# A retention layer with a mixture of adapters: 64-token chunks, attention products on four 64x64 array tiles, pairs of units in a fixed program order

## The chip, the core and the metric

The kernel runs on one core of one Trainium2 chip. A core has five engines with queues of their own: PE (TensorE, matrix products; the loads of its stationary operand are listed as PEld), DVE (VectorE), ACT (ScalarE), POOL (GpSimd) and SP (SyncE, which here issues nearly all DMA transfers). SBUF is the working memory of 128 partitions; PE writes its results to PSUM, 8 banks of 512 fp32 values a partition. PE's array can be addressed as one 128x128 array, as two tiles (64 rows x 128 columns, or 128 x 64) or as four 64x64 tiles[...]. The metric is the device time of one execution in microseconds (us); lower is better.

## What is computed

Inputs q, k and v have 8 batches, 8 heads, 576 tokens and 64 elements a head, in fp32. Head h decays with its own gamma. The result of all heads is a row of 512 per token, and a mixture of 8 adapters of rank 16, the best two of them per token, is added to it.

```python
scores = np.matmul(q, k.transpose(0, 1, 3, 2)) / np.sqrt(64)
gamma = 1.0 - 2.0 ** (-5.0 - np.arange(8))
rel = pos[:, None] - pos[None, :]
Dmat = np.where(rel >= 0, gamma[:, None, None] ** rel, 0.0)
ret = np.matmul(scores * Dmat, v)
x = ret.transpose(0, 2, 1, 3).reshape(4608, 512)

logits = x @ w_gate                      # 512 x 8
topk = the two largest of 8 per token
w = softmax over these two
out = x + sum over the two: w * (x @ A[e]) @ B[e]     # A: 512 x 16, B: 16 x 512
```

## The kernel before

The 576 tokens are cut into four chunks of 128 and one of 64. Within a chunk the products are done directly (scores, a triangular mask, times v); what earlier chunks contribute is held in a state P of 64 x 64 per batch and head, which is multiplied by gamma^128 after each chunk. The decays are folded into q (tile `aqp`) and v (`gv`), so the mask is of zeros and ones (`tri`).

A unit is one chunk of two batches with all 8 heads: 16 full units of 128 tokens (order: chunk by chunk, four pairs of batches each) and 4 half units of 64 tokens at the end. Each unit passes these stages, each a function:

- `stage_T` (L229): q and k are transposed on PE by a product with a 64x64 identity, in the mode of two 64x128 tiles. The results are taken out of PSUM to qT by DVE (times `aqp`, L241) and to kT by ACT (L250).
- `stage_S` (L291, L302): scores, keys by queries, 128 x 128 for each head and batch, contracting over 64 elements: two 64x128 tiles. DVE masks them to `rt`.
- `stage_O` (L359, L373, L387): the state times q into `px` (four 64x64 tiles, 128 columns wide), and the new state product k by v into `pu` (two 128x64 tiles). DVE adds the old state (`pn`), POOL multiplies by the decay (L388). In half units the state times q goes into a tile of its own, `pq` (L341), and ACT copies it.
- `stage_R` (L408): v times the masked scores, added in PSUM to `px` (two 128x64 tiles); ACT copies `px` to `xT`. For half units this is L426, on four 64x64 tiles.
- `stage_Z` (L447): gate logits and all adapters' first products, `pz`, on the whole array; then routing on DVE (L460 to L479) with a sigmoid on ACT (L468) between, which ends in `zc`, the weighted codes in fp16.
- `stage_X`, `stage_B`, `stage_Y` (L493, L512, L533): codes transposed, `xT` transposed back into `po`, and the adapters' second product added to it in PSUM; ACT takes `po` out (L543) and SP stores it.

POOL scales v in place for a unit ahead (L197). Loads come in groups of four batches (`issue_full`, L127; 1 MB each of q, k and v, in runs of 256 bytes); each kind has three buffers of 1 MB, so a group's buffers are those of the group three before.

The order of the work is not the program's: the framework's scheduler orders the instructions on each engine by its own costs. So a transpose or a state product can be placed between products that wait for DVE. The 8 PSUM banks are one pool; a tile takes a bank that has come free and waits for its last reader.

The loop that the program states is this:

```python
    for t in range(NU):
        if t % 2 == 0:
            issue(t // 2 + 2)
        stage_S(t)
        if t + 1 < NU:
            scale_v(t + 1)
        stage_O(t)
        stage_R(t)
        if t + 1 < NU:
            stage_T(t + 1)
        if t > 0:
            stage_B(t - 1)
            stage_X(t - 1)
        stage_Z(t)
        if t > 0:
            stage_Y(t - 1)
```

Of the kernel before, what the change touches and what calls it, by code (L numbers as in the profile page):

```python
# [10 lines left out]
FP32 = mybir.dt.float32  # L11
# [7 lines left out]
def kernel(  # L19
# [28 lines left out]
    tri_np = (jj[None, :] >= jj[:, None]).astype(np.float32)  # L48
# [5 lines left out]
    for hp in range(HP):  # L54
# [11 lines left out]
        [ident32_np, tri_np, trih_np, gv_np, gvh_np, g128_np], axis=1  # L66
# [20 lines left out]
    tri = pack[:, 128:256]  # L87
    trih = pack[:, 256:320]
    gv = pack[:, 320 : 320 + H]
    gvh = pack[:, 320 + H : 320 + 2 * H]  # L90
    g128 = pack[:, 320 + 2 * H : 320 + 2 * H + HP]
# [19 lines left out]

    nat = {}

    def issue_full(c, qd, split):
        tiles = []
        for src, tag in ((q, "q32"), (k, "k32"), (v, "v32")):
            tiles.append((src, iop.tile([128, QUAD * H, Dh], FP32, tag=tag, name=tag)))
        parts = ((0, 2), (2, 4)) if split else ((0, 4),)
        for lo, hi in parts:
            for src, tl in tiles:  # L120
                if split and lo == 0 and src is k:
                    nc.sync.dma_start(out=aqp, in_=dr_aqp.ap())
                if split and lo == 0 and src is v:
                    nc.sync.dma_start(out=pack, in_=dr_rest.ap())
                if split and lo == 2 and src is q:
                    load_moe()
                nc.sync.dma_start(  # L127
                    out=tl[:, lo * H : hi * H, :],
                    in_=src[
                        QUAD * qd + lo : QUAD * qd + hi, :, 128 * c : 128 * c + 128, :  # L130
                    ].rearrange("b h j d -> j (b h) d"),
                )
        for half in range(2):
            nat[(c, 2 * qd + half)] = [
                tl[:, half * 2 * H : half * 2 * H + 2 * H, :] for _, tl in tiles
            ]

    def issue_half(qd):

        s0 = 128 * NFULL  # L140
        tiles = []
        for src, tag in ((q, "q32"), (k, "k32"), (v, "v32")):
            tiles.append((src, iop.tile([128, QUAD * H, Dh], FP32, tag=tag, name=tag)))
        for slot in range(2):
            for src, tl in tiles:
                for par in range(2):
                    b = QUAD * qd + 2 * slot + par
                    nc.sync.dma_start(
                        out=tl[64 * par : 64 * par + LH, slot * H : slot * H + H, :],
                        in_=src[b, :, s0 : s0 + LH, :].rearrange("h j d -> j h d"),  # L150
                    )
            nat[(NFULL, 2 * qd + slot)] = [
                tl[:, slot * H : slot * H + H, :] for _, tl in tiles
            ]

    quads = [(c, qd) for c in range(NFULL + 1) for qd in range(NQ)]

    def issue(n):
        if n < len(quads):
            c, qd = quads[n]  # L160
            if c < NFULL:
                issue_full(c, qd, n == 0)
            else:
                issue_half(qd)

    issue(0)

    issue(1)
    nc.vector.tensor_copy(out=ident16, in_=ident32)
    gdec = cpool.tile([128, HP, 2, Dh], FP32, tag="gdec", name="gdec")  # L170
# [4 lines left out]
    P = [  # L175
        cpool.tile([128, HP, 2, Dh], FP32, tag=f"P{bp}", name=f"P{bp}")
        for bp in range(NP)
    ]

    def swap_aw():  # L180
        for ho in range(2):
            nc.gpsimd.tensor_copy(
                out=AW[1][64 * ho : 64 * ho + 64],
                in_=AW[0][64 - 64 * ho : 128 - 64 * ho],
            )

    units = [(c, 2 * qd + s) for c, qd in quads for s in range(2)]
    st = {}

    def scale_v(t):  # L190
        c, bp = units[t]
        full = c < NFULL
        v32 = nat[(c, bp)][2]
        nb = 2 if full else 1
        g = gv if full else gvh
        for b in range(nb):
            nc.gpsimd.tensor_tensor(  # L197
                out=v32[:, b * H : b * H + H, :],
                in0=v32[:, b * H : b * H + H, :],
                in1=g.unsqueeze(2).broadcast_to((128, H, Dh)),  # L200
                op=ALU.mult,
            )

    def stage_T(t):
        c, bp = units[t]
        full = c < NFULL
        q32, k32, v32 = nat[(c, bp)]
        qT = wk.tile([128, HP, 2, 128], FP32, tag="qT", name="qT")
        kT = wk.tile([128, HP, 2, 128], FP32, tag="kT", name="kT")
        L = 128 if full else LH  # L210
        for src, dst, nm in ((q32, qT, "q"), (k32, kT, "k")):
            dv = dst.rearrange("p a b i -> p a (b i)")[:, :, 0 : 2 * L].rearrange(
                "p a (b i) -> p a b i", i=L
            )
            if full:
                ps = [
                    pp.tile([128, HP, 2, 64], FP32, tag="pb", name=f"pt_{nm}")
                    for _ in range(2)
                ]
            else:  # L220
                ps = [
                    pp.tile([128, HP, 64], FP32, tag="pb", name=f"pt_{nm}")
                    for _ in range(2)
                ]
            for hp in range(HP):
                for b in range(2 if full else 1):
                    for r in range(2):
                        sl = slice(64 * r, 64 * r + 64)
                        nc.tensor.matmul(  # L229
                            ps[r][:, hp, b, :] if full else ps[r][:, hp, :],  # L230
                            lhsT=src[sl, b * H + 2 * hp : b * H + 2 * hp + 2, :],
                            rhs=id64[sl, :],
                            is_transpose=True,
                            start=True,
                            stop=True,
                        )
            for r in range(2):
                if full:
                    o = dv[:, :, :, 64 * r : 64 * r + 64]
                    if nm == "q":  # L240
                        nc.vector.tensor_tensor(  # L241
                            out=o,
                            in0=ps[r],
                            in1=aqp[:, :, 64 * r : 64 * r + 64]
                            .unsqueeze(2)
                            .broadcast_to((128, HP, 2, 64)),
                            op=ALU.mult,
                        )
                    else:
                        nc.scalar.copy(out=o, in_=ps[r])  # L250
                else:
                    o = dv[:, :, r, :]
                    if nm == "q":
                        nc.vector.tensor_tensor(
                            out=o, in0=ps[r], in1=aqp[:, :, 0:64], op=ALU.mult
                        )
                    else:
                        nc.scalar.copy(out=o, in_=ps[r])
        view = lambda tl: tl.rearrange("p a b i -> p a (b i)")[:, :, 0 : 2 * L].rearrange(
            "p a (b i) -> p a b i", i=L  # L260
        )
        st[t] = {"qT": view(qT), "kT": view(kT), "v": v32, "k": k32}

    def stage_S(t):
        c, bp = units[t]
        full = c < NFULL
        s = st[t]
        qT, kT = s["qT"], s["kT"]
        L = 128 if full else LH
        rt = {}  # L270
        hpg = 2 if full else 4
        for g in range(HP // hpg):
            ps = [
                pp.tile(
                    [128, hpg, 2, 128] if full else [128, hpg, LH],
                    FP32,
                    tag="pb",
                    name=f"ps_s{ho}",
                )
                for ho in range(2)  # L280
            ]
            for a in range(hpg):
                hp = g * hpg + a
                for b in range(2):
                    for ho in range(2):
                        sl = slice(64 * ho, 64 * ho + 64)
                        if full:
                            o = ps[ho][:, a, b, :]
                        else:
                            o = ps[ho][64 * b : 64 * b + 64, a, :]  # L290
                        nc.tensor.matmul(  # L291
                            o,
# [6 lines left out]
            for ho in range(2):  # L299
# [16 lines left out]
                for a in range(hpg):  # L316
                    rt[2 * (g * hpg + a) + ho] = r[:, a, :, :]
# [293 lines left out]
```

## Time and profile before

| | |
|---|---|
| median of 3 runs | 207.6 us (207.38 to 208.12) |
| span of the profiled execution, from the first to the last instruction | 205.1 us |
| mean granted PE clock | 0.995 |
| HBM read, written | 29.32 MB, 9.44 MB |
| mask L302, DVE, 128x512 | 64 times, 682 ns |
| q scaling L241, DVE, 128x512 | 32 times, 686 ns |
| new state L387, DVE, 128x512 | 12 times, 691 ns |
| copy of `px` L417 and of k L250, ACT, 128x512 | 32 times each, 585 and 589 ns |
| output copy L543, ACT, 128x256 | 72 times, 375 ns |
| scaling of v L197, POOL, 128x512 | 36 times, 1042 ns |
| decay of the state L388, POOL, 128x512 | 16 times, 1271 ns |
| store of 256 KB, issue to landing | 3.2 us |
| DMA share and rate, 50 to 60 us | 0.97, 277 GB/s |
| the same, 150 to 160 us | 0.52, 137 GB/s |

The median is of separate runs; the durations come from one profiled execution, whose span leaves out what lies before its first and after its last instruction. A group's mean is the duration of one instruction by itself; two of them in a row overlap a little (two copies of k take 1.07 us together). PE's matmuls overlap far more, so that their pace is read from the distance of their starts, or from the chain of waits, and not from their mean durations.

### The profile page before, as it was taken

The page shows a single profiled execution, that of the slowest core. Times are in us where ns is not written, and L with a number is a line of the kernel's source. Part 1 is how long each engine was busy: PE and PEld are TensorE (multiplying, and loading weights), DVE is VectorE, ACT ScalarE, POOL GpSimd, SP SyncE. Part 2 cuts the span into 40 slices and gives each one's busy share as a digit, 9 for nine tenths or more (in the row PEclk, how much of TensorE's full clock was granted, in tenths as well). Part 3 has the DMA queues.
Part 4 walks back from the last instruction along what each step waited for, and adds up shares of the span by engine and source line. Part 5 has one row for each costly group of instructions (what it writes and reads, how often), then busy time and mean ns, then how long its engine had stood idle before and what let it go on. Part 6 is the DMA issues. An engine that isn't in the chain of part 4 may idle for free.

```text
span 205.1 us, 8039 instructions
## 1 busy us (share of the span) xinstructions
PE 183.8 (90%) x3564; PEld 166.2 (81%) x3564; DVE 108.7 (53%) x286; ACT 76.6 (37%) x206; POOL 59.6 (29%) x60
## 2 busy tenths in 40 slices
PE   0476989799999999999999999999999999999950
PEld 0376969598999999999999999999999899888830
DVE  0226364937374746465656565656565655456630
ACT  2022324153525262625252525253434344454430
POOL 1144323521818202727202720643222402000000
PEclk9999999999999999999999999999999999999997
DMA  5989999799998988991799969756545311222222
GB/s 114 277 109 246 249 243 280 194 290 290 253 319 245 261 249 274 284 297 36 220 286 254 266 215 293 213 145 179 150 118 158 96 51 60 101 79 76 58 47 61
DMA packets 57442, 39.14 MB, mean 191 GB/s; under 512 B 30912, under 2 KB 52672, under 8 KB 57408
## 3 DMA queue, kind: packets, MB, share of 16 engines
q1 hardware_dynamic: 57264, 38.50, 68.0%
q8 instruction: 28, 0.46, 0.9%
q0 software_dynamic: 144, 0.13, 0.4%
q14 instruction: 6, 0.05, 0.1%
HBM read 29.32 MB, written 9.44 MB: 189 GB/s over the span
## 4 chain that ended last, share of the span: by engine, by line
PE 72%; SPq 9%; DVE 7%; DMA 5%; ACT 3%; issue 1%; ACTq 0%
PE pz L447 16%; PE px L408 12%; PE ps_s L291 12%; PE pu L373 6%; PE px L359 6%; PE pt_q L229 5%; DMA k<-in_k_dram 5%; PE po L512 4%; SPq L127 4%; PE pt_k L229 4%; PE po L533 3%; DVE rt L302 2%; PE px L426 2%; ACT osb L543 2%; SPq L101 2%; PE pzt L493 2%
## 5 line engine op out<-in xcount | busy, mean ns | idle before, releaser
L197 POOL TENSOR_TENSOR v<-v,pack 128x512 f32<-128x512 f32 x36 | 36.6, 1042 | 28.0 <-DMA v<-in_v_dram 28.0
L417 ACT COPY xT<-px 128x512 f32<-128x512 f32 x32 | 18.7, 585 | 66.0 <-PE px L408 66.0
L388 POOL TENSOR_TENSOR P<-pn,gdec 128x512 f32<-128x512 f32 x16 | 20.3, 1271 | 75.3 <-DVE pn L387 58.9
L302 DVE TENSOR_TENSOR rt<-ps_s,pack 128x512 f32<-128x512 f32 x64 | 39.7, 682 | 4.2 <-PE ps_s L291 4.2
L291 PE MATMUL ps_s<-qT,kT 64*128 64x128 f32 (+1 forms) x640 | 37.4, 275 | 1.2 <-ACT kT L250 1.2
L447 PE MATMUL pz<-AW,xT 128*128 128x136 f32 x288 | 37.8, 283 | 0.4 <-ACT zT L498 0.4
L291 PEld LDWEIGHTS ps_s<-qT,kT 64*128 64x128 f32 (+1 forms) x640 | 33.7, 184 | 5.3 <-DVE lg L460 3.4
L241 DVE TENSOR_TENSOR qT<-pt_q,aqp 128x512 f32<-128x512 f32 x32 | 20.6, 686 | 31.1 <-PE pt_q L229 31.1
L408 PE MATMUL px<-rt,v 128*64 128x128 f32 x512 | 34.1, 275 | 1.8 <-DVE rt L302 1.7
L447 PEld LDWEIGHTS pz<-AW,xT 128*128 128x128 f32 x288 | 34.7, 190 | 0.6 <-ACT zT L498 0.5
L543 ACT COPY osb<-po 128x256 f32<-128x256 f32 x72 | 23.1, 375 | 25.8 <-PE po L533 25.8
L408 PEld LDWEIGHTS px<-rt,v 128*64 128x64 f32 x512 | 29.0, 137 | 3.8 <-DVE rt L302 2.5
L250 ACT COPY kT<-pt_k 128x512 f32<-128x512 f32 x32 | 17.2, 589 | 19.2 <-PE pt_k L229 19.2
L460 DVE COPY lg<-pz 128x16 f32<-128x16 f32 (+1 forms) x20 | 3.5, 173 | 35.0 <-PE pz L447 35.0
L229 PE MATMUL pt_q<-id,q 64*128 64x64 f32 x288 | 13.6, 234 | 6.7 <-DMA q<-in_q_dram 6.7
L373 PE MATMUL pu<-v,k 128*64 128x64 f32 x512 | 18.9, 225 | 0.0
L373 PEld LDWEIGHTS pu<-v,k 128*64 128x64 f32 x512 | 16.5, 137 | 2.7 <-issue 2.1
L229 PEld LDWEIGHTS pt_q<-id,q 64*128 64x128 f32 x288 | 10.8, 142 | 9.6 <-issue 9.4
L229 PE MATMUL pt_k<-id,k 64*128 64x64 f32 x288 | 12.8, 228 | 3.4 <-DMA k<-in_k_dram 3.4
L473 DVE SCALAR_TENSOR_TENSOR cm<-lg,m,sg 128x8 f32<-128x8 f32 x36 | 9.9, 294 | 8.8 <-ACT sg L468 8.8
L229 PEld LDWEIGHTS pt_k<-id,k 64*128 64x128 f32 x288 | 10.9, 143 | 3.8 <-issue 1.7
L359 PE MATMUL px<-qT,P 64*64 64x128 f32 x384 | 13.2, 275 | 0.0
(34 smaller groups left out, 139.9 us busy)
## 6 DMA issues: line engine op xcount, KB each, us to landing
out_dram<-osb SPq DMA_DIRECT2D x32, 256.0 KB, 3.2
q<-in_q_dram SPq DMA_DIRECT2D x2, 512.0 KB, 5.0
k<-in_k_dram SPq DMA_DIRECT2D x2, 512.0 KB, 6.0
v<-in_v_dram SPq DMA_DIRECT2D x2, 512.0 KB, 5.4
q<-in_q_dram SPq DMA_DIRECT2D x8, 128.0 KB, 3.4
k<-in_k_dram SPq DMA_DIRECT2D x8, 128.0 KB, 3.3
v<-in_v_dram SPq DMA_DIRECT2D x8, 128.0 KB, 4.1
out_dram<-osb SPq DMA_DIRECT2D x8, 128.0 KB, 2.4
```

Of the source, the lines that this page charges most:

```text
L197: nc.gpsimd.tensor_tensor(out=v32[:, b * H : b * H + H, :], in0=v32[:, b * H : b * H + H, :], in1=g.unsqueeze(2).broadcast_to((128, H, Dh) ...
L229: nc.tensor.matmul(ps[r][:, hp, b, :] if full else ps[r][:, hp, :], lhsT=src[sl, b * H + 2 * hp : b * H + 2 * hp + 2, :], rhs=id64[sl, :], ...
L241: nc.vector.tensor_tensor(out=o, in0=ps[r], in1=aqp[:, :, 64 * r : 64 * r + 64] .unsqueeze(2) .broadcast_to((128, HP, 2, 64)), op=ALU.mult,)
L291: nc.tensor.matmul(o, lhsT=kT[sl, hp, b, :], rhs=qT[sl, hp, b, :], start=(a == 0 and (b == 0 or not full)), stop=True, skip_group_check=True,)
L302: nc.vector.tensor_tensor(out=r.rearrange("p a b i -> p (a b) i"), in0=ps[ho].rearrange("p a b i -> p (a b) i"), in1=tri.unsqueeze(1).broa ...
L359: nc.tensor.matmul(px[b][64 * cc : 64 * cc + 64, hp, :], lhsT=P[bp][64 * ho : 64 * ho + 64, hp, b, :], rhs=qT[64 * ho : 64 * ho + 64, hp, ...
L373: nc.tensor.matmul(pu[64 * ho : 64 * ho + 64, hp, b, :], lhsT=s["k"][:, b * H + h, :], rhs=s["v"][:, b * H + h, :], start=(hp == 0 and b = ...
L388: nc.gpsimd.tensor_tensor(out=pf, in0=pn, in1=gdec.rearrange("p a b d -> p (a b d)"), op=ALU.mult,)
L408: nc.tensor.matmul(px[b][64 * cc : 64 * cc + 64, hp, :], lhsT=s["v"][:, b * H + h, :], rhs=rt[h][:, b, :], start=(c == 0 and hp == 0), sto ...
L417: nc.scalar.copy(out=xt, in_=px[b])
L447: nc.tensor.matmul(pz[:, b, :], lhsT=xts[b][:, dt, :], rhs=AW[b][:, dt, :], start=(dt == 0), stop=(dt == HP - 1), skip_group_check=True,)
L543: nc.scalar.copy(out=osb[:, b, :, cc ^ b, :], in_=po[cc][:, b])
```

## The change

Every group of four batches of a 128-token chunk is now worked on as a pair of units (A and B, two batches each), and the last 64 tokens of all eight batches are a single pair. There is one chunk loop of nine rounds; the loads of a round lie two rounds ahead.

Within a 128-token chunk the work is cut into two halves of 64 tokens, s = 0 and 1. Each half has its own scores (64 x 64), its own state product, and a state of its own: P for the first half, and p1 = P + the first half's product for the second (`mid_state`); `end_state` adds the second half's product. So the scores between the halves are no longer formed, and in their place is a state product more. Contractions and outputs are all 64 wide: scores, state product, values times scores and state times q run on four 64x64 tiles with 64 columns each, twice as many instructions as before. The half tokens' pair uses the same functions without the state product.

A round goes through three array modes: four 64x64 tiles for all attention products of A and B, then two 64x128 tiles for the transposes of the next pair and of the previous pair's output, then the whole array for the codes' transposes, the gates and the adapters. The context `tc.manual_schedule()` keeps each engine's instructions in the program's order.

The state times q is now added after the values, into the same banks from other row tiles; for this a copy of one column by ACT (`see`) waits for the values, and the first product of the state waits for it. The copy `xT` interleaves the tokens of the two batches (i, b), so that a tile holds 64 tokens of two batches, and a store of 256 KB goes to 64 rows of each batch.

The routing writes the sigmoid's argument for both halves in one instruction (`ar`), so one sigmoid and one `zc` serve a unit where there were two. The 128 x 128 mask is dropped from the constants; k's first half is loaded ahead of the constants, and the second half of the first group ahead of the adapters' weights.

The core of the diff; the old stage functions, which stand above, are left out:

```diff
+    order = ctx.enter_context(tc.manual_schedule())
+    groups = [(c, qd) for c in range(NFULL) for qd in range(NQ)] + [(NFULL, 0)]
...
+    def stage_S(u):
+        ps = [
+            pp.tile([128, HP, 2, 64], FP32, tag="pb", name=f"ps_s{ho}") for ho in range(2)
+        ]
+        for hp in range(HP):
+            for b in range(2):
+                for s in range(2):
+                    for ho in range(2):
+                        sl = slice(64 * ho, 64 * ho + 64)
+                        ts_ = slice(64 * s, 64 * s + 64)
+                        nc.tensor.matmul(
+                            ps[ho][64 * s : 64 * s + 64, hp, b, :],
+                            lhsT=u.kT[sl, hp, b, ts_],
+                            rhs=u.qT[sl, hp, b, ts_],
...
+    def stage_U(u):
...
+                        nc.tensor.matmul(
+                            u.pu[s][64 * ho : 64 * ho + 64, hp, b, :],
+                            lhsT=u.k[sl, b * H + h, :],
+                            rhs=u.v[sl, b * H + h, :],
...
+    def mid_state(u):
+        p1 = wk.tile([128, HP, 2, Dh], FP32, tag="p1", name="p1", bufs=3)
+        if u.c == 0:
+            nc.vector.tensor_copy(out=flat(p1), in_=flat(u.pu[0]))
+        else:
+            nc.vector.tensor_tensor(
+                out=flat(p1), in0=flat(u.pu[0]), in1=flat(P[u.bp]), op=ALU.add
+            )
+        u.Ps = [None if u.c == 0 else P[u.bp], p1]
+
+    def end_state(u):
+        pn = wk.tile([128, HP, 2, Dh], FP32, tag="pn", name="pn")
+        nc.vector.tensor_tensor(
+            out=flat(pn), in0=flat(u.pu[1]), in1=flat(u.Ps[1]), op=ALU.add
+        )
...
+    def stage_R(u):
...
+                        cc = ho ^ s
+                        nc.tensor.matmul(
+                            u.px[s][64 * cc : 64 * cc + 64, hp, b, :],
+                            lhsT=u.v[sl, b * H + h, :],
+                            rhs=u.rt[ho][sl, hp, b, :],
...
+    def see(u):
+        w = mo.tile([128, 1], FP32, tag="see", name="see")
+        u.seen = nc.scalar.copy(out=w, in_=u.px[1][:, HP - 1, 1, 63:64])
+
+    def stage_Q(u):
...
+                        m = nc.tensor.matmul(
+                            u.px[s][64 * cc : 64 * cc + 64, hp, b, :],
+                            lhsT=u.Ps[s][sl, hp, b, :],
+                            rhs=u.qT[sl, hp, b, 64 * s : 64 * s + 64],
...
+                        if first:
+                            tc.add_manual_dep(m.ins, u.seen.ins.name, done, reason="rows")
...
+    def copy_x(u):
+        for s in range(2):
+            xt = mo.tile([128, HP, 128], FP32, tag="xT", name="xT", bufs=10)
+            nc.scalar.copy(
+                out=xt.rearrange("p a (i b) -> p a b i", b=2), in_=u.px[s]
+            )
...
+        nc.vector.scalar_tensor_tensor(
+            out=ar, in0=lg, scalar=2.0, in1=ns.unsqueeze(2).broadcast_to((128, 2, E)),
+            op0=ALU.mult, op1=ALU.subtract,
+        )
+        nc.vector.tensor_tensor(
+            out=ge, in0=lg, in1=m8[:, :, 1:2].broadcast_to((128, 2, E)), op=ALU.is_ge
+        )
...
+    for n in range(NG):
+        A_, B_ = G[n]
+        load(n + 2)
...
+        stage_S(A_)
+        mask(A_)
...
+        stage_S(B_)
+        mask(B_)
+        if A_.full:
+            for u in (A_, B_):
+                stage_U(u)
+                mid_state(u)
+        for u in (A_, B_):
+            stage_R(u)
+            see(u)
+        stage_Q(A_)
+        stage_Q(B_)
+        if A_.full:
+            for u in (A_, B_):
+                end_state(u)
+        if nxt:
+            scale_v(nxt[0])
+            scale_v(nxt[1])
+        if A_.full:
+            for u in (A_, B_):
+                decay(u)
+        copy_x(A_)
+        copy_x(B_)
+
+        if nxt:
+            stage_T(nxt[0], "q")
+            stage_T(nxt[0], "k")
+        if prev:
+            stage_B(prev[0])
+        if nxt:
+            stage_T(nxt[1], "q")
+            stage_T(nxt[1], "k")
+        if prev:
+            stage_B(prev[1])
+
+        if prev:
+            stage_X(prev)
+        stage_Z(A_)
+        route1(A_)
+        if prev:
+            stage_Y(prev[0])
+            evac(prev[0], 0)
+        sig(A_)
+        route2(A_)
+        if prev:
+            evac(prev[0], 1)
+        stage_Z(B_)
...
+            for u in prev:
+                for s in range(2):
+                    store(u, s)
+    A_, B_ = G[NG - 1]
+    stage_B(A_)
+    stage_B(B_)
+    for u in (A_, B_):
+        stage_X([u])
+        stage_Y(u)
+        for s in range(2):
+            evac(u, s)
+            store(u, s)
```

## The prediction

> **What bounds the kernel now.** I read the page's busy shares first, then the chain of waits in the steady part, then the timeline of the last stage and of SP's queue.
>
> ```profile
> span 205.1 us, 8039 instructions
> PE 183.8 (90%) x3564; PEld 166.2 (81%) x3564; DVE 108.7 (53%) x286; ACT 76.6 (37%) x206; POOL 59.6 (29%) x60
> ...
> DMA  5989999799998988991799969756545311222222
> ...
> q1 hardware_dynamic: 57264, 38.50, 68.0%
> ```
>
> PE is busy 90% of the span and nothing else is near it, but the row of DMA shares (40 slices) stands at 9 through most of the first half: a faster PE meets the DMA queue there. A busy PE need not be a full one, so next the chain between 113 and 124 us, one unit (start us, us, what):
>
> ```profile
> 113.56 1.91 PE pz L447 x16
> 115.47 0.44 PE po L533 x4
> 115.91 1.98 PE ps_s L291 x32
> 117.89 1.03 PE px L359 x32
> 118.93 1.08 PE pu L373 x32
> 120.01 1.77 PE px L408 x32
> 121.78 0.64 PE pt_q L229 x16
> 122.43 0.50 PE pt_k L229 x16
> 122.92 0.50 PE po L512 x16
> 123.42 0.22 PE pzt L493 x2
> ```
>
> No other engine appears: PE alone sets 10.07 us per unit, 20.1 per pair. Four of the ten pieces, the attention products, take 5.86 us. An fp32 matmul stands as two records (8 instructions of L447, x16), a transpose as one. The rows q and k of L229 are the same 16 records, yet q takes 0.64 and k 0.50: q comes first after L408, in another array mode, so a mode switch costs about 0.15. A unit passes five.
>
> The last stage (four half units) already runs the form that the change uses everywhere. In its timeline (start, us, engine, line):
>
> ```profile
> 186.69 0.56 PEld L291 LDWEIGHTS ps_s<-qT,kT 64*64 64x64 f32 x32 [0.21 <-issue]
> ...
> 187.15 1.03 PEld L341 LDWEIGHTS pq<-qT,P 64*64 64x64 f32 x32
> ```
>
> L291 puts 32 records of 64x64 on all four 64x64 tiles; the next line begins 187.15-186.69 = 0.46 us later, 14.4 ns a record. L341 uses the two tiles of the diagonal alone: 1.03 us, 32 ns a record. This pair of rows carries the forecast.
>
> SP's queue (start, us spent issuing):
>
> ```profile
> 20.58 4.24 SPq L127 DMA_DIRECT2D k<-in_k_dram  x1
> ...
> 46.30 0.94 SPq L127 DMA_DIRECT2D q<-in_q_dram  x1
> ...
> 61.96 0.71 SPq L127 DMA_DIRECT2D q<-in_q_dram  x1
> ...
> 77.92 0.71 SPq L127 DMA_DIRECT2D q<-in_q_dram  x1
> ```
>
> A group's loads and a pair's stores (3.1 + 1.0 MB) recur every 15.7 and 16.0 us there. The k of 20.58 is the second group's; in the chain its landing releases PE at 30.4.
>
> [...] Here cm (L473) has a median of 227 ns and a maximum of 1075, ns (L463) 161 and 1042[...].
>
> **PE, part by part, per steady pair.** Scores: 64 records a unit in place of 32, but half as wide and on four tiles: 64 x 14.4 = 0.92 for 1.98. State products: 64 x 14.4 = 0.92 for 1.08. Values times scores: 0.92 for 1.77. State times q: 0.92 for 1.03. Eight such stages a pair: 7.36. Unchanged in kind: four input transposes and two output ones, 6 x 0.50 = 3.00; gates 2 x 1.91 = 3.82; adapters 2 x 0.44 = 0.88; code transposes 0.22 + 2 x 0.06 = 0.34. Three switches a pair for ten; X's lies in its 0.22, the other two cost 0.30. Sum 15.70, against 20.1.
>
> **Does the cover hold?** Clock from the start of a pair's scores. PE would finish scores at 1.84, states 3.68, values 5.52, state times q 7.36, transposes from 7.5. A VectorE operation starts about 0.25 after PE's last record, as qT does after pt_q. VectorE first ends the previous pair's routing (logits, maxima, sigmoid, codes: about 2.2 us after its gates end, thus at 1.6), then four masks at 0.62 (2.48 x4 in the timeline): 2.84 and 4.08. PE wants them at 3.68 and 4.60: hidden, 0.5 spare. The added mid states (0.69 each) end at 5.5, wanted from 4.6+0.92 and 6.4; the end states at 6.8, wanted at 8.0 for their banks: hidden. Scaling q of the first next unit ends at 8.0+0.25+1.29 = 9.55; its bank is wanted by k of the second at about 9.45: 0.1 lost. The second's scaling ends at 10.95, wanted by the gates at 10.8: another 0.2. ScalarE: four copies of px from 6.7 at 0.54 end at 8.85, wanted at 9.0; k copies end at 10.0 and 11.4, the code copy near 12, wanted at 12.9. The two tiny copies "see" wait for R on ScalarE, with only the px copies queued behind them; each is over before its state product is due, since the other unit's product lies between. VectorE adds up to about 11.5 us a pair, ScalarE 9.3, GpSimd 4 x 1.04 + 2 x 1.27 = 6.7: none is the bound. The sigmoid and cm in one instruction a unit rather than two save time that is hidden: nothing.
>
> Costs that the trace does not show: the copy of px writes xT at every second element. Between 0 and twice its 0.54 (2.1 us a pair); I take 0, its count of elements being the same. The lock on four small routing operations: 0 to 2 us a pair if GpSimd scales v just then; v of the next group lands at other phases, so 0.2. Instruction supply: 64 records at 14.4 ns have no precedent beyond 32 in a row; 0 to 1 us a pair, and I take 0, since the wide stretch at 186.69 shows no gap. So a pair takes 15.7 + 0.3 + 0.2 = 16.2.
>
> **DMA.** Bytes and packet sizes stay; queue 1's 68.0% of 205.1 us is 139.5 us for 38.5 MB, hence 15.2 per pair's 4.19 MB, below 16.2 by one. Program order on SP: stores of the pair before last, then loads of the group two ahead. These start at about a pair's beginning and are wanted 1.5 pairs later (24 us): hidden. The front order moves k ahead of aqp and the second half of v ahead of the adapter weights; everything ahead of the second group's k is the same, so PE waits to 30.4 as before.
>
> **The sum.** From 30.4: three transposes 1.5, switch, gates 3.8, switch: scores of the second pair at 36.0 (34.2 before: its gates ran in the wait). That pair has a state product on two tiles only, 2 x 1.03: 16.4. The third group's k, by 37.85 + 5.5 = 43.4, meets a transpose at 44. Six pairs at 16.2: half stage at 149.6, where before reached it at 176.0. Half stage: without state products the first mask is waited for (values at 2.95 rather than 1.84), then 13.2 us to the end of its eighth step, 1.1 for both output transposes, and codes, copy, product and four evictions twice in a row: 20.0 in all (24.2 before). After the last eviction 4.9 us passed before; two stores of 256 KB land in 3.2 instead of 2.4: 5.7. So 149.6 + 20.0 + 5.7 = 175.3 of span against 205.1. The median of 207.6 lies 2.5 above the span; 175.3 + 2.5 = 177.8 us.
>
> **Rivals.**
> - Fixed order stalls (0.16). For: PE's queue is in order, with only 0.1 to 0.5 us to spare at masks and copies, where the scheduler of before had other work to put in. Against: each wait found above is under 0.3. At 17.5 to 19 a pair, 9 to 20 us more: 187 to 198.
> - DMA becomes the bound (0.08). For: shares of 9 up to 100 us, a period of 15.7 to 16.0. Against: that period held stores waiting for evictions. At 17.2 a pair, 7 us more: 185.
> - Four tiles do not hold 14.4 ns over 500 records (0.07), because weights or instructions do not come at one each 7 ns. For: no row is longer than 32. Against: L359 alternates the same four tiles at 1.03 for twice the width. At twice that, 28.8 ns, each stage doubles: 7 x 7.4 + 5.5 more, about 235. It decides from 30 us over some 3,900 records, 7.7 ns more: 22 ns a record. That is the case of slower.
> - The forecast (0.69): 173 to 184.
>
> **Range and chances.** 171 to 192 covers the forecast with its bounds, DMA and half of the stalls. Within 0.3% is about what a measurement of this kernel can tell from no change. Faster 0.91 (all but the third rival and the far end of the first), same 0.01, slower 0.08.
>
> **What would show it.** After: the four attention lines at 0.92 us per 64 records; scores of successive pairs 16.2 us apart; PE near 5,600 records, and three switches a pair; the chain of waits mostly PE from 45 us on, with DMA only before; second pair at 36, half stage at 150. Wrong if rows on four tiles exceed 20 ns a record, if the chain shows VectorE or ScalarE each pair, or if loads end the wait of transposes after 50 us.

## The result, and the profile after

The changed kernel is slower: a median of 235.0 us over four runs (229.2 to 239.3) beside 207.8 us (207.4 to 208.1). Times of one kernel scatter, so this ratio and the later ones compare only the runs within 1.5% of each kernel's fastest, here 229.2 and 231.7 us: 1.109, with a 95% interval of 1.102 to 1.116. The profiled execution has a span of 230.0 us against 205.1. The forecast was 177.8 us.

The page of the changed kernel, lines of its parts 1 to 3 (busy us, share and count; granted TensorE clock in 40 slices; queues with packets, MB and share):

```profile
span 230.0 us, 12085 instructions
...
PE 166.9 (73%) x5612; PEld 156.3 (68%) x5612; DVE 98.0 (43%) x250; ACT 73.4 (32%) x192; POOL 59.6 (26%) x60
...
PEclk9999999889995999999977999769997999999996
...
q1 hardware_dynamic: 57008, 38.44, 59.2%
q8 instruction: 44, 0.72, 1.3%
```

PE is busy 73% of the time where it was 90%: something else holds it. No other engine has grown and the data queue's share fell, so none of these has become the bound by its busy time. Two lines stand out. The clock row dips below 9 in five places before its end (before: in none). And queue 8, which looks like nothing at 1.3%, carries 44 packets of 16,384 bytes: 44 x 256 = 11,264, just over the 2 x 5612 = 11,224 instructions of PE (weight loads and products). By this count a packet is a block of 256 PE instructions, 64 bytes each. The kernel before had the same queue, with 28 packets for 2 x 3564 = 7128 instructions:

```profile
q8 instruction: 28, 0.46, 0.9%
```

What PE waited for between 36 and 205 us (us in total, times, longest):

```profile
PE px L317 <- issue: 12.8, 6, 3.3
PE px L346 <- issue: 12.2, 6, 3.8
PE pu L275 <- issue: 8.1, 5, 2.1
PE pu L275 <- DVE zc L407: 2.7, 1, 2.7
```

"issue" means that no semaphore explains the wait. The one data wait of some size, for zc, occurs once. PE's timeline in the fifth pair (start, us, what, and in brackets the idle time before it) shows where the pauses lie:

```profile
105.87 2.09 PE L243 MATMUL ps_s<-qT,kT 64*64 64x64 f32 x128
107.79 2.17 PE L275 MATMUL pu<-v,k 64*64 64x64 f32 x125
...
112.02 1.98 PE L317 MATMUL px<-rt,v 64*64 64x64 f32 x120 [1.89 <-issue]
...
116.30 0.37 PE L346 MATMUL px<-qT,P 64*64 64x64 f32 x2 [2.18 <-issue]
...
116.57 0.32 PE L346 MATMUL px<-qT,P 64*64 64x64 f32 x2
...
116.67 0.32 PE L346 MATMUL px<-qT,P 64*64 64x64 f32 x2
```

Scores of both units take 1.92 us for 128 records; the forecast had 1.84. The pauses come in the middle of lines, not where one stage needs another: 8 records into the values, 8 into state times q. From 112.02 to the next pause are 120 + 8 = 128 products, with their weight loads 256 instructions: one block. The last two rows, 0.10 us apart for four records (a row of L346 with the other tile name lies between them), are at 26 ns a record: the clock is halved there (the trace grants 0.5 from 116.2 to 119.6 us).

Counted over the trace: scores of the second pair begin at 36.48 us and those of the half pair at 204.85, seven periods of 24.05 us; the forecast had 36.0 and 149.6, so they took 54.8 us more in all. In this stretch PE pauses by over 0.25 us at 22 ends of blocks, which lie multiples of 256 instructions apart, 42.1 us together (a pause is counted here from the start of the last instruction before it to the start of the next, so it is some 0.2 us longer than the idle time in brackets); 2.7 is the wait for zc; about 10 remain, which stand beside 27.3 us at half clock.

### The profile page after: what moved, and what is told of

Same layout as the page of the kernel before. It is cut to its first block, busy times and chain, and to the rows that moved or that the text cites. A ratio compares the mean times of both kernels' runs of the same rounds, so it can differ in the third digit from the quotient of the medians.

```text
span 230.0 us, 12085 instructions
## 1 busy us (share of the span) xinstructions
PE 166.9 (73%) x5612; PEld 156.3 (68%) x5612; DVE 98.0 (43%) x250; ACT 73.4 (32%) x192; POOL 59.6 (26%) x60
## 5 line engine op out<-in xcount | busy, mean ns | idle before, releaser
L304 POOL TENSOR_TENSOR P<-pn,gdec 128x512 f32<-128x512 f32 x16 | 20.3, 1278 | 86.6 <-PE px L346 86.6
L317 PE MATMUL px<-rt,v 64*64 64x64 f32 x1152 | 23.4, 231 | 13.6 <-issue 13.4
L317 PEld LDWEIGHTS px<-rt,v 64*64 64x64 f32 x1152 | 21.6, 146 | 14.8 <-issue 14.6
L463 ACT COPY osb<-po 128x256 f32<-128x256 f32 x72 | 22.8, 372 | 21.0 <-PE po L451 20.4
L275 PE MATMUL pu<-v,k 64*64 64x64 f32 x1024 | 20.8, 233 | 11.3 <-issue 8.1
L362 ACT COPY xT<-px 128x512 f32<-128x512 f32 x36 | 20.5, 633 | 24.2 <-PE px L346 24.2
L275 PEld LDWEIGHTS pu<-v,k 64*64 64x64 f32 x1024 | 19.0, 146 | 12.4 <-issue 11.8
L346 PE MATMUL px<-qT,P 64*64 64x64 f32 x512 | 19.3, 243 | 10.8 <-issue 10.8
L346 PEld LDWEIGHTS px<-qT,P 64*64 64x64 f32 x512 | 17.6, 156 | 11.5 <-issue 11.5
L346 PE MATMUL px<-qT,p 64*64 64x64 f32 x512 | 21.4, 243 | 4.5 <-issue 4.5
L211 PE MATMUL pt_q<-id,q 64*128 64x64 f32 x288 | 15.7, 261 | 10.4 <-DMA q<-in_q_dram 7.9
L346 PEld LDWEIGHTS px<-qT,p 64*64 64x64 f32 x512 | 19.6, 156 | 4.9 <-issue 4.9
L243 PE MATMUL ps_s<-qT,kT 64*64 64x64 f32 x1152 | 21.7, 230 | 1.3 <-ACT kT L230 1.3
L243 PEld LDWEIGHTS ps_s<-qT,kT 64*64 64x64 f32 x1152 | 19.8, 144 | 3.7 <-ACT kT L230 2.1
```

The lines of the kernel that those rows point to most:

```text
L211: nc.tensor.matmul(ps[r][:, hp, b, :], lhsT=src[sl, b * H + 2 * hp : b * H + 2 * hp + 2, :], rhs=id64[sl, :], is_transpose=True, start=Tru ...
L243: nc.tensor.matmul(ps[ho][64 * s : 64 * s + 64, hp, b, :], lhsT=u.kT[sl, hp, b, ts_], rhs=u.qT[sl, hp, b, ts_], start=(hp == 0 and b == 0) ...
L275: nc.tensor.matmul(u.pu[s][64 * ho : 64 * ho + 64, hp, b, :], lhsT=u.k[sl, b * H + h, :], rhs=u.v[sl, b * H + h, :], start=(hp == 0 and b ...
L304: nc.gpsimd.tensor_tensor(out=flat(P[u.bp]), in0=flat(u.pn), in1=flat(gdec), op=ALU.mult)
L317: nc.tensor.matmul(u.px[s][64 * cc : 64 * cc + 64, hp, b, :], lhsT=u.v[sl, b * H + h, :], rhs=u.rt[ho][sl, hp, b, :], start=(hp == 0 and b ...
L346: m = nc.tensor.matmul(u.px[s][64 * cc : 64 * cc + 64, hp, b, :], lhsT=u.Ps[s][sl, hp, b, :], rhs=u.qT[sl, hp, b, 64 * s : 64 * s + 64], s ...
```

## The experiments

The theory after reading this: **supply**. PE gets its instructions in blocks of 256, a block can't come faster than some 4 us (an estimate: the 22 that PE waited for above began 4.26 us after the block before on the mean), and stages on four tiles use one up in 1.9. Rivals: **loads** (the blocks are late because the DMA engines are busy with data), **tiles** (the array doesn't hold 14.4 ns over long stretches), **order** (waits and mode switches of the fixed program order), **clock** (the throttle comes first, the rest follows).

### PE alone, without and with loads

`rest` gives products of the full array, 512 wide; `stream` a count of products on four 64x64 tiles, of a width, from a bank on.

```diff
+    rest(16)
+    stream(512, 64, 0)
+    rest(12)
+    stream(256, 128, 2)
+    rest(12)
+    stream(192, 192, 0)
+    rest(12)
+    stream(128, 256, 2)
```

> Leaves out the whole computation: PE alone multiplies one loaded block in four streams of fp32 products on the four 64x64 tiles, 512 products 64 wide (1024 records, 2048 instructions), 256 products 128 wide, 192 products 192 wide, 128 products 256 wide, each after a stretch of full-array products; no load runs beside them. Only the streams' times are read. Supply (PE gets its instructions in blocks of 16 KB, 256 instructions, at best one per about 3.9 us): the 64-wide stream takes 26 to 31 us in place of 15, with pauses of about 2 us every 256 instructions; the 128-wide one (3.7 us of array work a block) 15 to 17 with small pauses or none; 192 and 256 wide 16.6 and 14.8 without a pause. Loads (the blocks are late because the DMA engines are busy with loads): no pauses, the 64-wide stream 15 us. Tiles (the array or its weight loads do not hold 14.4 ns over long stretches): about 30 us, spread evenly over its records, with no pauses at multiples of 256. Clock alone (the throttle comes first): no pauses, records of 29 ns from the point at which the clock is halved.

> The same streams (the computation is left out) with 24 loads of 1 MB beside them. Supply: the same pauses as without the loads, a block coming per 3.9 to 5 us, the 64-wide stream 28 to 40 us; the 128-wide one may now pause by 0.5 to 1 us a block. Loads: pauses only here, and over 1.5 times the stream's time without loads. Tiles: as without the loads, about 30 us spread evenly.

Each of the two ran once. PE's timeline without loads; the last row is the 128-wide stream:

```profile
24.94 3.02 PE L57 MATMUL bank<-w 64*64 64x64 f32 x191
29.09 2.09 PE L57 MATMUL bank<-w 64*64 64x64 f32 x128 [1.13 <-issue]
32.55 2.09 PE L57 MATMUL bank<-w 64*64 64x64 f32 x128 [1.36 <-issue]
36.00 2.09 PE L57 MATMUL bank<-w 64*64 64x64 f32 x128 [1.36 <-issue]
...
61.68 14.24 PE L57 MATMUL bank<-w 64*64 64x128 f32 x512
```

Nothing is loaded, nothing is waited for, the granted clock is 1.00, and every 128 products PE stops. A block takes 3.45 us, of which 1.87 are work (14.6 ns a record). The 128-wide stream, whose blocks are 3.55 us of work (four in 14.2), runs without a pause, and so do the wider ones. The stream of 64 took from 24.94 to 51.19, 26.2 us in place of 15. Tiles and clock fall here, and loads as the sole cause. The expected 3.9 us a block was too high.

The same with loads beside it:

```profile
34.04 3.46 PE L57 MATMUL bank<-w 64*64 64x64 f32 x128 [6.21 <-issue]
38.59 2.09 PE L57 MATMUL bank<-w 64*64 64x64 f32 x128 [1.09 <-issue]
43.69 3.52 PE L57 MATMUL bank<-w 64*64 64x64 f32 x128 [3.01 <-issue]
48.79 2.09 PE L57 MATMUL bank<-w 64*64 64x64 f32 x128 [1.58 <-issue]
```

Now a block takes 5.0 us on the average of those after the first, which took 8.3, and the 128-wide stream pauses as well (PE was busy 16.1 of the 20 us from 80 to 100, in which most of it lies, at a granted clock of 1.00). Rows of 3.5 us are at half clock (the stretch had 13.7 us of it): the clock fell during the long pauses or just after them. So both hold: a floor without loads, and loads that raise it.

The packets of queue 8, set against the starts of PE's instructions, split the floor; a block counts as asked for when its packet starts. Means over the blocks that PE waited for, in us, from the first instruction of a block on:

```
                        until its     the      from landing to the    sum
                        successor is  fetch    successor's first
                        asked for              instruction
stream, no loads        1.06          1.02     1.38                   3.46
stream, loads           2.63          1.27     1.53                   5.4
changed kernel          1.85          1.07     1.34                   4.26
```

In the stream without loads PE asks for the next block only about 1.1 us after it has begun the present one. Each of the waits in the table ended 1.1 to 1.8 us after the landing of the packet that was asked for during the block just before, so no second block lay in stock. PE had one block of look-ahead in these traces and no more: a stretch with few instructions saved nothing up for a dense one behind it. Loads lengthened the asking (up to 5.6 us in the stream, 3.9 in the changed kernel), and the fetch far less (1.27 us for 1.02). Without loads the crossing of a block's end cost 1.6 us, where a block is worked off in 1.9.

### The gates put between the attention stages

```diff
+        if prev:
+            stage_Z(prev[0], 0)
         if A_.full:
             for u in (A_, B_):
                 stage_U(u)
                 mid_state(u)
+        if prev:
+            stage_Z(prev[0], 1)
+            route1(prev[0])
...
```

> The changed kernel's instructions, with the previous pair's gates put in fours between the four attention groups: scores, gates, state products, gates, values, gates, state times q, gates. Eight more mode switches a pair (1.2 us), no instruction fewer or more. Supply: each attention group (512 instructions, two blocks) stands beside 1.9 us of gates with few instructions, so pauses shrink and the clock is halved less: a pair falls from 24.0 to 20 to 22.5 us, in all 205 to 222. Order and switches (dependency waits of the fixed order or the switches are the cost): 25 or more a pair, 236 to 245. Tiles or clock alone: the same work at the same pace, 229 to 236.

The first profile had pairs of 20.5 to 22.6 us from the third on and a span of 215.0, as the supply theory had it; but its four times were 216.8, 228.1, 231.4 and 234.4, and their median of 229.8 lies where tiles or clock alone had been expected. So it ran again, beside the changed kernel.

> The changed kernel once more, as a partner on the same chip for the three others. 229 to 239, pairs about 24 us apart.

> The spread order once more, since its first four times ran from 216.8 to 234.4 although its profile showed pairs of 21.6 us. Supply: the lowest of its times lies 10 us or more under the changed kernel's lowest beside it, and its median too lies under the changed kernel's. Order and switches: its lowest is no lower than the changed kernel's, the first profile having been an exception.

Changed kernel: 226.2 to 236.9, median 234.1. Spread: 224.5 to 241.9, median 233.1. Neither expectation came true as written: the lowest is lower by 2 us, not by 10, and over both sets of runs the two kernels can't be told apart by time. The waits tell what happened. Spread, first profile (34 to 186 us), then the second (34 to 203), PE's waits:

```profile
PE po L452 <- ACT zT L426: 5.2, 7, 0.8
PE px L317 <- issue: 4.8, 7, 2.0
```

```profile
PE px L317 <- issue: 8.1, 6, 2.4
PE pt_q L211 <- DVE zc L408: 6.5, 3, 3.5
```

Pauses at ends of blocks fell from 42.1 and 44.6 us (the two profiles of the changed kernel) to 21.5 and 27.3: that part of the theory held twice. But the order that thins the stages out made adapters wait for their codes (5.2 us) and transposes for zc (6.5 in the second profile, 1.8 in the first), and in the second profile the clock was halved for 23.9 us, in the first not at all. The gain was given back to new waits of the order and, in some executions, to the clock. What the clock followed is worked out below; why some executions have longer pauses than others was not settled.

### No loads in the changed kernel

```diff
     def load(n):
         if n >= NG:
             return
+        if n >= 3:
+            nat[n] = nat[n - 3]
+            return
```

> The changed kernel without the loads from the fourth group on: those groups compute on the data of the first three again (the output of those tokens isn't the reference's), with every instruction of PE kept. Supply alone (a block of instructions comes as late without loads): pairs stay near 24 us, 225 to 235. Supply slowed by the loads (3.5 us a block with idle DMA engines, 5.0 beside loads, as the two streams showed): from the fifth pair on 17.6 (5.1 blocks at 3.46) to 20 us a pair, in all 195 to 208. Loads alone: no pauses are left, 16.2 a pair, 185 to 190. Order or tiles: 229 and more.

219.6 us median, ratio to the kernel before 1.053 (1.047 to 1.059): between the cases. One window of its profile (busy us and count of PE, PEld, DVE, ACT, POOL, then clock, DMA share, GB/s) and PE's waits from 62 to 195 us:

```profile
100.00:120.00 20.00, 16.58 (x639) 15.42 (x638) 9.28 (x27) 7.27 (x21) 5.53 (x6) 1.00 0.16 57
```

```profile
PE px L320 <- issue: 9.9, 6, 2.3
PE pu L278 <- issue: 8.8, 6, 2.0
PE px L349 <- issue: 7.6, 5, 1.9
```

With the DMA engines at 0.16 and the clock at 1.00 the pauses are still there: 33.3 us over six pairs, 5.5 a pair. Pairs are 22.1 us apart on the mean of six. The expectation of 17.6 to 20 took the floor as an average, 5.1 blocks at 3.46; that was its mistake. With the one block of look-ahead that the traces show, the dense part counts alone: the eight attention stages are 8 x 128 = 1024 instructions, four blocks, 4 x 3.45 = 13.8 us in place of 7.36, and the rest of a pair keeps its 15.7 - 7.36 = 8.3: 22.1. That is the measured number, though so close a match is partly chance: the sum leaves out the switches, and the six pairs had 6.8 us at half clock, which can account for up to 0.6 us a pair. Of the 7.8 us a pair that the changed kernel lost, about 5.9 are there without loads, nearly all of it the floor, and about 1.9 are what loads and the clock add.

### Half of the units back in the old form

In each pair the first unit computes 128-token chunks with the products of the kernel before, the second 64-token chunks on four tiles.

```diff
+            stage_U64(B_)
+            mid_state(B_)
+            stage_Q128(A_)
+            stage_R(B_)
+            see(B_)
+            stage_U(A_)
+            end_state(A_)
+            stage_Q(B_)
+            end_state64(B_)
+            stage_R128(A_)
+            copy_x(B_)
```

> In each pair the first unit in the 128-token form, the second in four-tile 64-token form, its stages put between those of the first: 524 matmul records a pair (1048 instructions, 4.1 blocks) between 396 and 652. Array work is about 17.8 us a pair with seven switches. Supply at 4.2 us a block (between idle and loaded) needs 17.2: hidden, pairs of 17.8 to 18.8, in all 190 to 198, faster than both kernels. Supply at 5.0: 20.5 a pair, 205 to 212. Order or tiles: over 212, half of what the changed kernel lost.

> The hybrid without the loads from the fourth group on (later groups compute on the first three groups' data again, their output isn't the reference's). Supply with one block of look-ahead (the next block is asked for about 1.1 us after the first instruction of a block ran, lands 1.0 later, runs 1.4 later, 3.45 in all without loads; with loads the asking alone took up to 4.1 us): its dense part, three blocks in 10 us, just fits, pauses of at most 0.6 us a block stay, pairs of 18 to 19.4 us from the fifth on, in all 199 to 208. Order (the hybrid's own dependency waits and seven switches cost it the 4 us a pair): as with the loads, 215 to 222.

With loads: 220.2 us median, ratio 1.059 (1.052 to 1.066), worse than either number of the supply theory and in the range that order or tiles had been given (over 212), so that only the run without loads could tell them apart; pairs 19.6 to 25.2 us apart. Without: 207.0, ratio 0.995 (0.992 to 0.999), pairs of 18.9 to 20.3 from the fifth on. The expectation with loads had been made before the look-ahead was known, again with an average over the pair; the one without was made with it and held in its total, while the last two of the four pairs took 19.9 and 20.3 and pauses there reached 0.7. The rival, the order's own waits and switches at 215 to 222, falls. PE's waits with loads (60 to 194 us), then without (60 to 177):

```profile
PE pu L313 <- issue: 4.7, 2, 3.0
PE pt_q L217 <- issue: 2.4, 1, 2.4
```

```profile
PE px L385 <- issue: 0.9, 1, 0.9
PE px L423 <- issue: 0.6, 2, 0.4
```

The program is the same, its order and its switches too; only the loads differ. Single waits of 2 to 3 us shrink below 1, and no other wait takes their place. Its dense part is three blocks in 10 us of work: 3.45 a block just fits, the 4.3 measured beside loads doesn't.

### All full units in the old form, in the new order

```diff
+            stage_Q128(A_)
+            stage_Q128(B_)
+            stage_U(A_)
+            end_state(A_)
+            stage_U(B_)
+            end_state(B_)
+            stage_R128(A_)
+            stage_R128(B_)
```

> The changed kernel's pairs and fixed order, but full units in 128-token chunks with the forms of the kernel before: scores on two tiles of 64x128, state times q on four tiles 128 wide, state products and values on 128x64; five switches a pair in place of ten of the kernel before, 396 matmul records a pair in place of 652; the half pair as in the changed kernel. Supply: no pauses; 20.1 less five switches and what unit-wise order lost, 18.8 to 19.6 a pair, 195 to 203 in all, faster than both. Order (the fixed order's own waits cost the time): at least 22 a pair, 215 or more. Tiles: 195 to 203 as well.

205.8 us, ratio 0.995 (0.990 to 1.000), span 204.4. Undoing the four-tile form of the full units takes back the whole loss, with pairs, program order and fused codes kept: it is not the order that costs 27 us. But it missed its 195 to 203. The full pairs have no pause at a block's end; PE's waits from 57 to 179 us are one line:

```profile
PE ps_s L245 <- ACT osb L523: 0.7, 2, 0.3
```

The last pairs are 19.5 us apart as expected, the early ones 20.1 to 20.8, mostly because scores take longer there (4.0 to 4.7 us in place of 3.8), in part waiting for their banks. The half pair, still on four tiles, takes 9.7 us for scores, values and state times q, where the array needs 5.5 (by estimate: six stages of 0.92): three dense blocks again. And the five switches fewer bring 0.48 us a pair (19.60 beside twice 10.04 a unit), 0.1 each if the whole difference is put down to them.

> The 128-token order with three waits of its trace removed, no form changed: the first pair's gates run before the transposes that wait for the second group (3.4 us), ScalarE evicts both outputs of a unit before the next sigmoid so that the scores' banks come free earlier (0.9 us in each of four pairs), and in the half pair the previous pair's transposes, codes and adapters stand between the dense four-tile stages (2 us of the 3.4 that these waited for instructions). Supply: no block falls under its floor in the full pairs, 195 to 200, faster than both kernels. Rival (the waits only move): 202 to 206.

The last hunk stands between scores and values of the half pair.

```diff
+        if n == 0:
+            gate(A_)
+            gate(B_)
...
             evac(prev[1], 0)
+            evac(prev[1], 1)
             sig(B_)
...
+            for u in prev:
+                stage_B(u)
+            stage_X(prev)
```

200.2 us, ratio 0.970 (0.965 to 0.974): faster than both kernels, just above its range of 195 to 200. Its page and PE's waits from 51 to 175 us:

```profile
span 198.3 us, 7994 instructions
...
PE 177.1 (89%) x3564; PEld 165.8 (84%) x3564; DVE 110.9 (56%) x266; ACT 71.2 (36%) x176; POOL 59.3 (30%) x60
...
q8 instruction: 28, 0.46, 1.0%
```

```profile
PE ps_s L245 <- DVE zc L467: 1.2, 3, 0.6
PE pu L306 <- issue: 0.3, 1, 0.3
```

28 blocks in place of 44, and one wait for instructions of 0.3 us left in the full pairs. In the half pair, which still waits for them twice (0.2 and 0.8 us), the same three four-tile stages with transposes, codes and adapters between them take 10.3 us, where they and those pieces summed to 12.0; the second pair begins at 34.0 instead of 37.4. Some scores still wait for a bank (4.5 to 5.1 us in three pairs in place of 3.8), some 3 of the 5 us by which it stayed above 195.

## Why the prediction was wrong

- **The failed step.** "Instruction supply: 64 records at 14.4 ns have no precedent beyond 32 in a row; 0 to 1 us a pair, and I take 0, since the wide stretch at 186.69 shows no gap." The step saw the risk and priced it from too short a piece of evidence. That stretch is 64 instructions; the block of 256 that holds it took 5.0 us in the kernel before, so it could show no gap. The term measured 6.0 us a pair in pauses (42.1 over seven), and its bound of 1 excluded that.
- **What the trace of before had to say.** Queue 8 stood in the page with 28 packets, one per 256 instructions of PE. From 34 us to the half pair no block was worked off in less than 4.9 us there, and the successor was asked for as late as some 3 us after a block's start. The forecast of 16.2 us a pair for 1304 instructions asks for a block every 3.2 us, and in the attention stages every 1.9. Both were beyond anything that trace showed.
- **The third rival** named instructions that "do not come at one each 7 ns" and put 235 us on it, with a chance of 0.07. Its number is the measured median, by luck; its mechanism fits only in part. It doubled the pace of every attention stage evenly, 29 ns a record. In fact the tiles keep 14.6 ns a record and PE stands still at the ends of blocks, which matters for the cure: wider products had no pauses (the 128-wide stream without loads), and work with few instructions between the dense stages shortened them (21.5 and 27.3 us for 42.1 and 44.6).
- **Clock.** No term of the sum allowed for it. The pauses come first: the stream without loads has them, 1.6 us in every 3.45, at full clock. In the changed kernel half clock came for 3.4 or 6.8 us at a time, each time during a pause or within 1.3 us of its end, but not after every pause. In the windows before it PE was still busy for 0.3 to 1.7 us. The traces show where the line runs. Their clock changes on a grid of 3.413 us: in the changed kernel's, the 13 spells of one clock between 24.1 and 225.5 us last 1, 2, 6, 12 or 14 times that. In all twelve traces, from 15 us to PE's last product, 593 windows of that grid began at full clock. The 26 in which PE (weight loads counted) was busy for up to 1.51 us were all followed by half clock, six of the 31 with 1.53 to 1.90 were, and none of the 536 busier ones. The stream without loads has 2.05 in most windows and just keeps its clock; with loads it had windows of 0.4 to 1.0. So the clock followed the pauses. About 10 us of the 54.8 are left for it here, an estimate by what remains.
- **Four-tile pace.** Right: 14.6 ns measured in the stream for the 14.4 used, over 128 records in a row.
- **Cover of masks, states and copies.** Right in sum: between 36 and 205 us PE waited for VectorE or ScalarE 3.1 us, 2.7 of them once for zc; the copy to every second element of xT took 633 ns beside 585. What the forecast priced at 0.2 us as the lock on small routing operations shows in the traces as long ones beside GpSimd: before, the seven of L463 and L473 that took over 500 ns (524 to 1075) all ran while it scaled v or the state; after, ten did (685 to 1178), five of them between 35 and 42 us, ahead of the end of the one wait for zc. With PE slower than forecast the cover was not put to its test.
- **DMA hidden, starts and ends.** The second pair came at 36.48 for 36.0, rightly forecast. From the half pair to the end 25.1 us for 25.7 is luck: to the last output copy it took 21.4 us for 20.0, with waits of 0.6 and 1.5 us for instructions, and the stores behind it 3.8 for 5.7. So the seven pairs between hold the error of the total. No wait for data shows there. That loads could delay instructions, on a queue of 1.3%, was not thought of.
- **Switches.** 0.15 each was taken from one pair of rows; the 128-token order gives 0.1, by the difference above.
- **Fixed order (the first rival).** Not the cause: the order with the old form is at 0.995, and 0.970 after three repairs.

## What to carry to other kernels

Count instructions as a resource with a rate: for every 256 that PE issues in a row, ask whether their work lasts as long as the fetch of the next block (3.45 us here with idle DMA engines, 4.3 to 5 beside loads), and do it for the densest stretch, not on the average, since in these traces only one block was fetched ahead. Cutting work into smaller tiles that run side by side can raise the instruction rate more than it saves array time: here it doubled the attention instructions to cut 5.86 us of them to 3.68 (by estimate: 256 records at 14.4 ns). Without loads a block of 64-wide fp32 products on four tiles (1.87 us of work) was past the limit here and one of 128-wide products (3.55) just at it. In these traces the mark was idle time put down to "issue" in the middle of a line, at equal counts of 256 instructions. Pauses then cost twice: all 26 windows of 3.413 us in which PE worked for up to 1.51 us were followed by half clock.

## What the runs showed of the hardware that was not expected

- Where PE waited and nothing was loaded, a steady stream took 3.45 us from the first instruction of a block to the first of the next: 1.1 until it is asked for, 1.0 for 16 KB, 1.4 until it runs.
- Loads on the data queue delayed the asking, from 1.1 to 2.6 us on the mean and 5.6 at most in the stream, while the fetch itself grew from 1.0 to 1.3. By what path they delayed it stays open.
- Half clock came after windows in which PE was not idle: of the windows of 3.413 us that began at full clock, all with PE busy for up to 1.51 us led to it, and none with more than 1.90.
- Executions of a kernel that starves in this way scatter: 226 to 239 us for the changed one and 217 to 242 for the spread order, where the kernel before stayed within 1.7% in each set of runs and the repaired order within 0.7%.
